# wo and w1 in long rows, and a quarter of one wo block moved into mid-run, in a decode kernel of attention and a Mish MLP

## The chip, the cores and the metric

One core of a Trainium2 chip runs the kernel. The metric is the device time of one execution in microseconds. A core has a matrix engine (TensorE, PE in the profile, with its weight loads as PEld), a vector engine (VectorE, DVE), a scalar engine (ScalarE, ACT), GpSimd (POOL) and SyncE (SP), which here issues nearly all transfers. Sixteen DMA engines carry the data from HBM into SBUF, whose 128 partitions the engines read; results of matmuls land in PSUM.

## The reference, cut to what matters

One token for each of 8 sequences (B = 8) passes a layer norm, and then two branches side by side: grouped-query attention over a cache (32 query heads, 8 key/value heads, 8192 positions, head size 128), and a dense layer of 1792 with Mish and a dense layer back. Everything is float32.

```python
xn = _layernorm(x, axis=-1)                       # x: 8 x 1 x 512
q = (xn @ wq).reshape(B, Sq, 32, 128)             # wq: 512 x 4096
scores = q . k_cache * 128 ** -0.5                # k_cache, v_cache: 8 x 8 x 8192 x 128
o = softmax(scores) . v_cache
A = o.reshape(B, Sq, 4096) @ wo                   # wo: 4096 x 512
h = xn @ w1 + b1                                  # w1: 512 x 1792
M = (h * tanh(softplus(h))) @ w2                  # w2: 1792 x 512
return x + A + M
```

## The kernel before

The work is cut into 32 units. Unit j is one batch row b = j % 8 with one pair m = j // 8 of key/value heads (NP = 4 pairs). A unit has 8.39 MB of keys and as many of values, and each of these is one transfer of 128 rows of 64 KiB (`load_unit`). The query projection of a pair, `project`, needs a quarter of wq, which `load_q` brings into the 16 KiB tile `ws`; it is loaded at b = 4 of the pair before and used at b = 5.

One large tile `kv` holds everything else. Values lie in its first 64 KiB of each partition (V_AT). Keys of even and odd units lie in two 64 KiB places that overlap by half (K_AT), so that the keys of unit j + 1 may be issued when one half of the scores of unit j has been computed. w1, the input x and the scratch of the Mish part share the first key place (W1_AT). K0, the first unit's keys, is loaded to the place of the values, so V0 must wait for the scores of unit 0, and K2 must wait for the Mish scratch to be free.

The program is written in the order in which each engine runs it (a manual schedule): every engine takes its instructions in program order and waits on semaphores where it needs another's result. At the start come the constants, the layer norm on 8 partitions (lines 169 to 183), eight small transposes of the normalised x into PSUM tile `M` (lines 184 to 189: four with stride 4 for the projection, `xn4`; four of 128 neighbouring columns for w1, `xnT`), their copies out, four matmuls that spread x for the residual (line 193), then the projection of pair 0, `spread` and the key weights of unit 0.

The loop over units then does, for unit j: the scores (line 279) in two halves with the next keys' transfer issued between them; the softmax (`softmax`); the values of unit j - 1 (`values`, line 341) on the probabilities that were turned in the iteration before; the transfer of V_j, which overwrites V_(j-1) and so follows `values(j - 1)`; the key weights of unit j + 1; for j = 0 `mish`; for some j `load_q` and `project`; `turn`, which permutes the exponentials with matmuls and lets DVE transpose and reduce them into `pt8` (lines 318 to 329); and `merge(j - 1)`, which scales the output of unit j - 1 and puts it into `oT` (lines 358 and 359). SP's issues are in the same order: K_(j+1), V_j, wq if it is due. A matmul in float32 appears as two matmul entries and two weight-load entries in the profile. Matmuls whose results go to the four quarters of PSUM's partitions, as most here do, run four at a time.

`mish` adds b1 and multiplies x by w1 (line 370: 4 blocks of 128 input rows times 4 groups of 448 columns), applies Mish with 14 vector operations in a chain, and leaves the turned result in `aT` (line 404).

After the loop SP issues wo as four transfers of 2 MiB (one for each pair, lines 477 to 480: 128 partitions times four rows of 4 KiB) and w2 as four (line 486). PE computes the values of the last unit, then `outputs(m, ...)` for three pairs (line 413: 8 matmuls for each pair, straight from `oT`), `merge` of the last unit and the outputs of the fourth pair. ACT copies the sum out of PSUM, four matmuls fold it (line 497), `down` adds the product with w2 (line 425), DVE adds x, and one transfer writes the result.

Of the kernel before, what the change touches and what calls it, by code (L numbers as in the profile page):

```python
# [13 lines left out]
P = 128  # L14
# [35 lines left out]

W2R = 7
# [7 lines left out]
PLACES = 2 * ROW + ROW // 2  # L59

# [5 lines left out]
def kernel(  # L66
# [39 lines left out]
    xnT = const.tile([P, CC, B], F32, name="xnT")  # L106
    qr = const.tile([P, DI, H2 * B], F32, name="qr")
    xres = const.tile([P, P], F32, name="xres")
    oT = const.tile([P, NP, H2, B], F32, name="oT")
# [20 lines left out]
    low = kv[:B, W1_AT : W1_AT + 3 * D]  # L130
    x_sb, xc, sq = (low[:, i * D : (i + 1) * D] for i in range(3))
# [5 lines left out]
    w1_t = kv[:, W1_AT : W1_AT + 7168].rearrange("p (j f) -> p j f", j=2 * CC)  # L137
# [5 lines left out]
    nc.gpsimd.memset(pt8, 0.0)  # L143
    for t in (H, O, M):
        nc.vector.memset(t, 0.0)
# [7 lines left out]
    nc.vector.reduce_sum(bsel, ident.rearrange("p (g q) -> p q g", g=G), axis=AX.X)  # L153
    nc.vector.reduce_sum(hsel, ident.rearrange("p (c h) -> p h c", h=H2), axis=AX.X)
# [29 lines left out]
    for c in range(CC):  # L184
        nc.tensor.transpose(M[:, c * B : (c + 1) * B], xc[:, c::CC], ident[:B, :B])
    for c in range(CC):
        nc.tensor.transpose(
            M[:, 32 + c * B : 32 + (c + 1) * B], xc[:, c * P : (c + 1) * P], ident[:B, :B]
        )
    nc.vector.tensor_copy(xn4.rearrange("p c b -> p (c b)"), M[:, 0:32])  # L190
    nc.vector.tensor_copy(xnT.rearrange("p c b -> p (c b)"), M[:, 32:64])
# [21 lines left out]
    def project():  # L213

        w = ws.rearrange("p (c f) -> p c f", c=CC)
        for d in range(2):
# [8 lines left out]
            qp = work.tile([P, 512], F32, name="e")  # L225
# [63 lines left out]
    def softmax(j):  # L289
# [18 lines left out]
        e = E[j] = work.tile([P, 512], F32, name="e")  # L308
# [47 lines left out]
    def merge(j, os):  # L356
        m, b = divmod(j, B)
        nc.tensor.matmul(M[:, 168 : 168 + H2], os, hsel, start=True, stop=True)  # L358
        nc.vector.tensor_mul(oT[:, m, :, b], M[:, 168 : 168 + H2], RT.pop(j))


    def mish(w1_t, b1_sb, flat):
# [5 lines left out]
        for c in range(CC):  # L368
            for g in range(G):
                nc.tensor.matmul(  # L370
                    hp[Q * g : Q * g + B, :],
                    xnT[:, c, :],
                    w1_t[:, c * 2 + g // 2, g % 2 * FG : (g % 2 + 1) * FG],
                    start=False,
                    stop=(c == CC - 1),
# [31 lines left out]
    A = X[:, 0]  # L407

    def outputs(m, t):
        w = t.rearrange("p (u f) -> p u f", u=4)  # L410
        for d in range(2):
            for h in range(REP):
                nc.tensor.matmul(
                    A[Q * h : Q * h + B, :],
                    oT[:, m, d * REP + h, :],
                    w[:, d * 2 + h // 2, h % 2 * D : (h % 2 + 1) * D],
                    start=(m == 0 and d == 0),
                    stop=(m == NP - 1 and d == 1),
                )

    def down(lo, hi, w):
        for j in range(2 * lo, 2 * hi):
            for g in range(G):
                at = (j - 2 * lo) * D + g * P
                nc.tensor.matmul(
                    H[Q * g : Q * g + B, :P],
# [7 lines left out]
    nc.sync.dma_start(w1_t, w1.rearrange("j p f -> p j f"))  # L434
# [6 lines left out]
    for j in range(UNITS):  # L441
# [20 lines left out]
        if j == 0:  # L462
            mish(w1_t, b1_sb, kv[:, W1_AT : W1_AT + 6 * FG])
        if more and b == LOAD_Q:
            load_q(j // B + 1)
        if more and b == MAKE_Q:
            qT = project()
        turn(j, lsel)
        if j > 0:
            merge(j - 1, os)  # L470
        if more and b == SPREAD_Q - 1:
            selections()


    w_o = [kv[:, 4096 * m : 4096 * (m + 1)] for m in range(NP)]
    for m in range(NP):
        nc.sync.dma_start(
            w_o[m].rearrange("p (u f) -> p u f", u=4),
            wo[4 * m : 4 * (m + 1)].rearrange("u p f -> p u f"),
        )  # L480
    w2_rows = w2.rearrange("j p f -> (j p) f").rearrange("(q i) f -> q (i f)", i=W2R)
    w2_t = []
    parts = ((0, 2), (2, 4), (4, 6), (6, 7))
    for lo, hi in parts:
        t = kv[:, W2_AT + lo * BW : W2_AT + hi * BW]
        nc.sync.dma_start(t, w2_rows[:, lo * BW : hi * BW])  # L486
# [60 lines left out]
```

## Time and profile before

| | |
|---|---|
| median of 3 runs (lowest to highest) | 1312.56 us (1312.44 to 1312.78) |
| the profiled execution, its own time | 1312.45 us |
| its span, first to last instruction | 1310.7 us |
| busy: PE / DVE / ACT | 989.0 us (75%) / 515.1 us (39%) / 40.2 us (3%) |
| read from HBM | 561.01 MB, 428 GB/s over the span |
| mean granted clock of TensorE | 0.879 of full speed |

In the rows of the profile an instruction is named by its engine, the line of the program, the operation and `out<-in` with the tiles' names; then come partitions x elements and a count. In a timeline the first number is the start in us from the span's start, the second the duration, and in brackets stands how long the engine was idle before and what ended that. In the windows a row has a stretch of time, its length, the busy time (and number) of PE, PEld, DVE, ACT and POOL, the granted TensorE clock, the mean busy share of the 16 DMA engines, and GB/s. A share over 1 in a short window comes from packets that are counted where they begin. SPq stands for SP's queue of DMA issues.

### The profile page before, as it was taken

Reading aid. Unit: us, or ns where it says so; the run is one execution under the profiler, and the core shown is the slowest. Engines: PE = TensorE matmul, PEld = TensorE weight load, DVE = VectorE, ACT = ScalarE, POOL = GpSimd, SP = SyncE. Lnnn points to the kernel's source line nnn. Section 1 sums busy time; section 2 is a strip of 40 time slices with the busy share of each in tenths; the row PEclk is TensorE's granted clock in tenths of the full one; section 3 lists DMA queues with packets and bytes.
Section 4 is the critical chain, followed back from the end, with each engine's and each line's share of the span. In section 5 each row is a group of like instructions: output and inputs, shape, how many; then the busy total and the mean of one; then the engine's idle time right before and its main releaser. Section 6 shows DMA issues by size and latency. Waiting matters only on the chain.

```text
span 1310.7 us, 11149 instructions
## 1 busy us (share of the span) xinstructions
PE 989.0 (75%) x5040; PEld 340.5 (26%) x5040; DVE 515.1 (39%) x728; ACT 40.2 (3%) x88; POOL 2.2 (0%) x9
## 2 busy tenths in 40 slices
PE   5978867768877668777878777687686678677676
PEld 3222222222322222232322222232232222222222
DVE  3364334432444442335243344414444433344421
ACT  1000000000000000000000000000000000000000
POOL 0000000000000000000000000000000000000000
PEclk9988888898888888877888888888898898888898
DMA  9999999999999999999999999999999999999997
GB/s 393 451 422 439 427 436 430 432 439 429 441 429 433 431 437 425 447 415 447 423 439 433 427 441 423 443 425 439 429 435 431 435 431 437 432 435 421 441 414 322
DMA packets 13735, 561.79 MB, mean 429 GB/s; under 512 B 1260, under 2 KB 1392, under 8 KB 4600
## 3 DMA queue, kind: packets, MB, share of 16 engines
q1 hardware_dynamic: 13664, 561.06, 99.3%
q8 instruction: 39, 0.64, 0.2%
q10 hardware_dynamic: 24, 0.02, 0.0%
q14 instruction: 8, 0.07, 0.0%
HBM read 561.01 MB, written 0.07 MB: 428 GB/s over the span
## 4 chain that ended last, share of the span: by engine, by line
DMA 72%; PE 23%; DVE 2%; SPq 2%; issue 0%; ACT 0%; DVEq 0%
DMA kv<-in_v 71%; PE o L341 20%; SPq L486 1%; DMA kv<-in_w 1%; PE s L279 1%; DVE pt L329 1%; PE x L244 1%; PE h L370 0%; PE m L229 0%; PE h L218 0%; DVE kv L392 0%; DVE tr L323 0%; DVE wk L262 0%; DVE nm L291 0%; ACT L177 0%
## 5 line engine op out<-in xcount | busy, mean ns | idle before, releaser
L279 PE MATMUL s<-kv,wk 128*64 128x512 f32 x2048 | 504.4, 655 | 174.6 <-DMA kv<-in_kT 171.9
L341 PE MATMUL o<-kv,pt 128*32 128x512 f32 x2048 | 268.6, 684 | 54.9 <-DMA kv<-in_v 45.3
L279 PEld LDWEIGHTS s<-kv,wk 128*64 128x64 f32 x2048 | 155.6, 151 | 498.0 <-issue 320.6
L329 DVE TENSOR_REDUCE pt<-tr 64x512 f32<-64x2048 f32 x64 | 241.3, 3771 | 1.6
L291 DVE TENSOR_REDUCE nm<-s 128x1 f32<-128x512 f32 x32 | 22.1, 691 | 366.7 <-PE s L279 366.7
L318 PE MATMUL x<-e,perm 128*128 128x512 f32 x256 | 128.4, 648 | 2.0 <-ACT qr L251 2.0
L341 PEld LDWEIGHTS o<-kv,pt 128*32 128x32 f32 x2048 | 69.9, 123 | 227.1 <-issue 169.6
L349 DVE TENSOR_SCALAR os<-o,isel 128x128 f32<-128x128 f32 x32 | 11.2, 351 | 274.8 <-PE o L341 274.8
L323 DVE STREAM_TRANSPOSE tr<-x 128x512 f32<-128x512 f32 x128 | 78.7, 673 | 0.0
L262 DVE TENSOR_TENSOR wk<-qr,mask 128x512 f32<-128x512 f32 x64 | 63.0, 1026 | 19.7 <-ACT qr L251 19.7
L318 PEld LDWEIGHTS x<-e,perm 128*128 128x128 f32 x256 | 50.0, 206 | 76.2 <-issue 73.7
L310 ACT ACTIVATE e<-s,nmx 128x512 f32<-128x512 f32 x32 | 22.0, 687 | 1095.7 <-DVE nmx L307 1095.7
L351 DVE SCALAR_TENSOR_TENSOR os<-o,isel,os 128x128 f32<-128x128 f32 x96 | 33.7, 351 | 3.4
L292 PE MATMUL m<-ident,nm 128*1 128x128 f32 x32 | 8.7, 273 | 29.8 <-DVE nm L291 29.8
L303 PE MATMUL m<-ident,nx 1*128 1x1 f32 x32 | 7.0, 219 | 24.1 <-DVE nx L299 24.1
L244 PE MATMUL x<-qT,tr 128*128 128x64 f32 x128 | 19.3, 315 | 3.0 <-ACT qr L251 2.7
L321 DVE RECIPROCAL rt<-m 128x8 f32<-128x8 f32 x32 | 6.6, 207 | 36.1 <-PE m L319 36.1
L244 PEld LDWEIGHTS x<-qT,tr 128*128 128x128 f32 x128 | 18.1, 226 | 6.2 <-ACT qr L251 3.3
L358 PE MATMUL m<-hsel,os 128*128 128x8 f32 x64 | 12.4, 266 | 9.3 <-DVE rt L321 9.3
L312 DVE TENSOR_SCALAR lsel<-rsel,l 128x8 f32<-128x8 f32 x32 | 7.4, 231 | 30.1 <-ACT e L310 30.1
L292 PEld LDWEIGHTS m<-ident,nm 128*1 128x1 f32 x32 | 2.5, 79 | 58.0 <-DVE nm L291 58.0
L319 PEld LDWEIGHTS m<-lsel,ones 128*128 128x128 f32 x64 | 12.2, 190 | 15.4 <-issue 15.1
(88 smaller groups left out, 163.9 us busy)
## 6 DMA issues: line engine op xcount, KB each, us to landing
ws<-in_wq SPq DMA_DIRECT2D x4, 2048.0 KB, 34.3
kv<-in_wo SPq DMA_DIRECT2D x4, 2048.0 KB, 24.3
kv<-in_w SPq DMA_DIRECT2D x1, 3584.0 KB, 26.4
kv<-in_w SPq DMA_DIRECT2D x3, 1024.0 KB, 19.3
kv<-in_kT SPq DMA_DIRECT2D x32, 29.9
kv<-in_v SPq DMA_DIRECT2D x32, 30.2
kv<-in_w SPq DMA_DIRECT2D x1, 512.0 KB, 19.5
out<-os SPq DMA_DIRECT2D x1, 64.0 KB, 1.6
```

The source lines that it names most:

```text
L244: nc.tensor.matmul(X[:, half, k * 64 : (k + 1) * 64], wide[:, half * 8 + k], qT, start=True, stop=True,)
L262: nc.vector.tensor_mul(w[:, :, d], q[:, :, d].to_broadcast([P, DI, NH * G, REP]), mask[:, d * NH * G : (d + 1) * NH * G] .rearrange("p (o ...
L279: nc.tensor.matmul(S[64 * c : 64 * (c + 1), :], w[:, i].rearrange("p d k h -> p (d k h)"), kk[:, i, c, :], start=(part == 0 and n == 0), s ...
L291: nc.vector.tensor_reduce(nm, S, axis=AX.X, op=ALU.max, negate=True)
L310: nc.scalar.activation(e, S, AF.Exp, bias=nmx, accum_out=l)
L318: nc.tensor.matmul(X[:, g], perm[:, g], e, start=True, stop=True)
L323: nc.vector.transpose(tr.rearrange("p (l t) c -> p t l c", t=TL)[:, tl], X.rearrange("p g (t q l) -> p t l g q", t=TL, q=PP)[:, tl],)
L329: nc.vector.tensor_reduce(pt8[half, :, :, d * REP : (d + 1) * REP].rearrange("p c y h -> p y c h"), tr[half].rearrange("p y (g c h) -> p y ...
L341: nc.tensor.matmul(O[Q * q : Q * (q + 1), :], pt8[:, c, TL * l : TL * (l + 1), :].rearrange("p t h -> p (t h)"), vt[:, 512 * n : 512 * (n ...
L351: nc.vector.scalar_tensor_tensor(os, O[:, DH * i : DH * (i + 1)], isel[:, i : i + 1], os, op0=ALU.mult, op1=ALU.add)
L358: nc.tensor.matmul(M[:, 168 : 168 + H2], os, hsel, start=True, stop=True)
L486: nc.sync.dma_start(t, w2_rows[:, lo * BW : hi * BW])
```

## The change

wo: the four transfers now read the same 2 MiB blocks as one run of memory, so that each partition gets one row of 16 KiB. A partition then holds four neighbouring rows of a block instead of row p of each of four, and the attention output must lie on the partitions in the same order: the new `turn_o(m)` does that for a pair with 16 matmuls by slices of the identity and one copy, `oT` into `oX`. For the first pair the row has 12 KiB only. The missing quarter (512 KiB) comes into `ws` by twelve transfers in mid-run (`load_few`): eight of three rows of 16 KiB at j = 22 to 25, to partitions p, p + 4 and p + 8 with p = 0 to 3 and 32 to 35, and four of two rows at j = 28 and 29, to partitions 0 to 7. Their matmuls are `few(0)` at the end of iteration 27 and `few(1)` after the last values; `turn_few` lays out their side of the product once, after unit 7. All of these add into PSUM tile `H`, which takes the place of `X` as accumulator of the outputs; the product with w2 goes to `O` in place of `H`.

w1: each partition reads one run of 28 KiB, eight rows of 896. The input must match: x is copied on 8 partitions into a new order (`xe`), turned by eight transposes and masked into two halves (`x8`), and `mish` has 32 matmuls for w1 where it had 16.

w2 comes in five parts (three of 8 KiB a partition, two of 2 KiB) in place of four. The work tile "e" has one buffer in place of two, and `project` comes after `turn` and `merge` in its iteration.

```diff
+W1R = 8
+FEW1 = [(32 * h + t, 3, 12 * h + t, 22 + (4 * h + t) // 2) for h in range(2) for t in range(4)]
+FEW2 = [(t, 2, 24 + t, 28 + t // 2) for t in range(4)]
+EARLY = 27
...
+    xe = kv[:B, W1_AT + 3 * D : W1_AT + 3 * D + W1R * P].rearrange("b (i s) -> b i s", i=W1R)
...
     for c in range(CC):
         nc.tensor.transpose(M[:, c * B : (c + 1) * B], xc[:, c::CC], ident[:B, :B])
+    nc.vector.tensor_copy(xn4.rearrange("p c b -> p (c b)"), M[:, 0:32])
     for c in range(CC):
-        nc.tensor.transpose(
-            M[:, 32 + c * B : 32 + (c + 1) * B], xc[:, c * P : (c + 1) * P], ident[:B, :B]
-        )
-    nc.vector.tensor_copy(xn4.rearrange("p c b -> p (c b)"), M[:, 0:32])
-    nc.vector.tensor_copy(xnT.rearrange("p c b -> p (c b)"), M[:, 32:64])
+        nc.vector.tensor_copy(
+            xe.rearrange("b i (c h q) -> b c i h q", c=CC, h=2)[:, c],
+            xc[:, c * P : (c + 1) * P]
+            .rearrange("b (o q i) -> b i o q", o=1, i=W1R)
+            .to_broadcast([B, W1R, 2, P // CC // 2]),
+        )
+    for i in range(W1R):
+        nc.tensor.transpose(M[:, 32 + i * B : 32 + (i + 1) * B], xe[:, i], ident[:B, :B])
+    for h in range(2):
+        nc.vector.tensor_scalar(
+            x8[:, :, h],
+            M[:, 32 : 32 + W1R * B].rearrange("p (i b) -> p i b", i=W1R),
+            hmask[:, h : h + 1],
+            None,
+            op0=ALU.mult,
+        )
...
-        nc.vector.tensor_mul(oT[:, m, :, b], M[:, 168 : 168 + H2], RT.pop(j))
+        nc.vector.tensor_mul(oT[:, :, b], M[:, 168 : 168 + H2], RT.pop(j))
+        if b == B - 1:
+            turn_o(m)
+        if j == B - 1:
+            turn_few()
+
+    def turn_o(m):
+        for i in range(CC):
+            for u in range(CC):
+                nc.tensor.matmul(
+                    M[Q * u : Q * (u + 1), 256 + 2 * B * i : 256 + 2 * B * (i + 1)],
+                    ident[:, i::CC],
+                    oT[:, 2 * u : 2 * u + 2].rearrange("p h b -> p (h b)"),
+                    start=True,
+                    stop=True,
+                )
+        nc.vector.tensor_copy(
+            oX[:, m].rearrange("p i h b -> p (i h b)"), M[:, 256 : 256 + 2 * CC * B]
+        )
...
-        for c in range(CC):
+        for i in range(W1R):
             for g in range(G):
                 nc.tensor.matmul(
                     hp[Q * g : Q * g + B, :],
-                    xnT[:, c, :],
-                    w1_t[:, c * 2 + g // 2, g % 2 * FG : (g % 2 + 1) * FG],
+                    x8[:, i, g // 2],
+                    w1_t[:, i, g % 2 * FG : (g % 2 + 1) * FG],
...
+    def load_few(p, n, q):
+        rows = wo[:4].rearrange("u p f -> (u p f)").rearrange("(u q i f) -> q u i f", u=4, i=4, f=BW)
+        nc.sync.dma_start(
+            ws[p : p + 4 * n - 3 : 4].rearrange("p (u f) -> p u f", u=4),
+            rows[q : q + 4 * n - 3 : 4, :, 3],
+        )
+
+    def turn_few():
+        o = oT.rearrange("p h b -> p (h b)")
+        n = H2 * B
+        for k, (p, m, lo) in enumerate(((0, 12, 0), (32, 12, 12), (0, 8, 24))):
+            part = k // 2
+            nc.tensor.matmul(
+                M[p : p + m, 384 + n * part : 384 + n * (part + 1)],
+                ident[:, 4 * lo + 3 : 4 * (lo + m) : 4],
+                o,
+                start=True,
+                stop=True,
+            )
+            nc.vector.tensor_copy(
+                oF[p : p + m, part].rearrange("p u h b -> p (u h b)"),
+                M[p : p + m, 384 + n * part : 384 + n * (part + 1)],
+            )
+
+    def few(part):
+        rows = (44, 8)[part]
+        for n in range(2 * CC):
+            nc.tensor.matmul(
+                H[Q * (n % G) : Q * (n % G) + B, :],
+                oF[:rows, part, n // 2, n % 2],
+                ws[:rows, n * D : (n + 1) * D],
+                start=(part == 0 and n < G),
+                stop=False,
+            )
...
-    nc.sync.dma_start(w1_t, w1.rearrange("j p f -> p j f"))
+    nc.sync.dma_start(w1_t, w1.rearrange("j p f -> (j p f)").rearrange("(p i f) -> p i f", p=P, i=W1R))
...
+        for p, n, q, at in FEW1 + FEW2:
+            if j == at:
+                load_few(p, n, q)
         if more and b == LOAD_Q:
             load_q(j // B + 1)
-        if more and b == MAKE_Q:
-            qT = project()
         turn(j, lsel)
         if j > 0:
             merge(j - 1, os)
+        if more and b == MAKE_Q:
+            qT = project()
         if more and b == SPREAD_Q - 1:
             selections()
+        if j == EARLY:
+            few(0)
...
-        nc.sync.dma_start(
-            w_o[m].rearrange("p (u f) -> p u f", u=4),
-            wo[4 * m : 4 * (m + 1)].rearrange("u p f -> p u f"),
-        )
+        rows = wo[4 * m : 4 * (m + 1)].rearrange("u p f -> (u p f)")
+        rows = rows.rearrange("(p f) -> p f", p=P)
+        n = 3 * BW if m == 0 else 4 * BW
+        nc.sync.dma_start(w_o[m][:, :n], rows[:, :n])
...
-    parts = ((0, 2), (2, 4), (4, 6), (6, 7))
+    parts = ((0, 4), (4, 8), (8, 12), (12, 13), (13, 14))
...
     os = values(UNITS - 1, v_t.pop(UNITS - 1))
+    few(1)
     for m in range(NP - 1):
         outputs(m, w_o[m])
     merge(UNITS - 1, os)
     outputs(NP - 1, w_o[NP - 1])
```

60 lines of the change are left out of this document (33 added, 27 removed).

## The prediction

> **What bounds the kernel now.** I read the page first, then the DMA share and rate by windows.
>
> ```profile
> span 1310.7 us, 11149 instructions
> ...
> q8 instruction: 39, 0.64, 0.2%
> ...
> DMA 72%; PE 23%; DVE 2%; SPq 2%; issue 0%; ACT 0%; DVEq 0%
> ...
> kv<-in_v SPq DMA_DIRECT2D x32, 30.2
> ```
>
> The chain that ended last is 72% DMA. Its 20% on L341 is a bookkeeping effect: while a unit's values run, the next keys are already moving. The windows decide (share of 16 engines, then GB/s):
>
> ```profile
> 200.00:400.00 200.00, 158.30 (x786) 54.82 (x781) 78.60 (x107) 6.23 (x14) 0.00 (x0) 0.86 1.00 433
> 29.00:35.00 6.00, 3.68 (x10) 1.21 (x12) 1.94 (x2) 0.29 (x1) 0.00 (x0) 1.00 1.03 412
> 1284.00:1296.00 12.00, 12.00 (x104) 2.88 (x96) 1.40 (x4) 0.00 (x0) 0.00 (x0) 0.89 1.03 412
> 1300.00:1301.00 1.00, 0.63 (x8) 0.00 (x0) 0.00 (x0) 0.26 (x1) 0.00 (x0) 1.00 0.58 242
> 1305.00:1306.00 1.00, 0.00 (x0) 0.00 (x0) 0.00 (x0) 0.00 (x0) 0.00 (x0) 1.00 0.34 139
> ```
>
> In mid-run all 16 engines are full at 433 GB/s (27.1 each). The stages with short rows are full too, but carry 412: w1 (29 to 35 us) and wo (1284 to 1296). In the last stretch only 0.58 of the engines work, so nine of the 16 end later than the other seven, by most of the time between 1299 and 1306: about 7 us. The 39 instruction packets of 16 KB are the only unequal load the page shows; 7 us against 39/9 of them is 1.6 us of lag for each. That cause is inferred. So the end is set by the late engines' bytes, and by any moment at which their queue is empty.
>
> **The change, part by part.** The times below are those of the profiled execution: 1312.45 us, 0.11 below the median of the three runs shown (1312.56), with 1.75 us outside its span.
>
> **Rows and the moved quarter: -2.1 us of transfers at the end, -0.4 at the start.** wo is 8.39 MB: at 412 GB/s 20.4 us. Afterwards 7.86 MB remain there; in 12 and 16 KiB rows at 433 that is 18.2 us (-2.2; if longer rows brought nothing, 7.86/412 is 19.1, -1.3). w1's 3.67 MB go from 8.9 to 8.5 us. w2's last 4 KiB part becomes two of 2 KiB: 0.1 us more at worst, since its four parts become five.
>
> **The few rows.** 512 KB go in twelve transfers. If each row has its own engine, two engines take twelve rows of 16 KiB (192 KB) and one takes eight. At 25.8 GB/s (412/16) 192 KB is 7.6 us. That is free as long as those engines are among the early seven with their 7 us; the excess of 0.6 us, less what the idle time below evens out, is taken as +0.5 (0 to 0.8). Their issues cost SP twelve times 0.33 us, in its idle time.
>
> **Start of the run: layer norm to w1.** Read the PE rows, and the DVE rows next to them:
>
> ```profile
> 9.96 0.57 PE L187 MATMUL m<-ident,kv 8*128 8x8 f32 x4
> 10.91 0.61 PE L193 MATMUL m<-kv,ident 8*8 8x128 f32 x8 [0.38 <-DVE xnT L191]
> ```
>
> ```profile
> 8.87 0.47 DVE L183 TENSOR_SCALAR kv<-kv,st 8x512 f32<-8x512 f32 x1
> 10.57 0.19 DVE L190 COPY xn<-m 128x32 f32<-128x32 f32 x1 [1.23 <-PE m L187]
> ```
>
> L193 waits for DVE's last read of M, and the projection is queued behind it. New in that path are four copies of 8x256 (between 0.19 and 0.47 each; near 0.3 as half of L183's elements, 1.2 in all), eight transposes in place of four, now after the copies and not beside them (0.11 to 0.14 each, 1.0), and two masked copies of 128x64 (0.2 each) where one copy stood. L190 itself comes after four transposes, not eight (-0.5). Sum about +2.0 us (1.3 to 3.0) for projection, spread and scores(0).
>
> **mish.** Sixteen more matmuls, 32 more entries:
>
> ```profile
> 51.10 4.79 PE L370 MATMUL h<-kv,xnT 128*8 128x448 f32 x32
> ...
> 79.93 9.62 PE L341 MATMUL o<-kv,pt 128*32 128x512 f32 x64
> ```
>
> ```profile
> 51.00:54.00 3.00, 2.90 (x16) 0.59 (x20) 0.50 0.81 350
> 54.00:55.90 1.90, 1.89 (x20) 0.36 (x12) 0.90 1.28 552
> ```
>
> The first 16 entries ran at a granted clock of 0.50 (0.18 us each), the rest at 0.90 (0.095). The new ones come last, so 32 x 0.095 = 3.0 us; at the low clock throughout 5.8. The bounds of the whole delay are thus 4.3 and 8.8, and I take 2.0 + 3.0 = 5.0.
>
> **Who waits for that.** K2 overwrites mish's scratch, and V1 overwrites V0:
>
> ```profile
> 67.46 0.22 DVE L404 COPY aT<-kv 128x112 f32<-128x112 f32 x1
> ```
>
> ```profile
> 67.75 0.33 SPq L123 DMA_DIRECT2D kv<-in_kT  x1
> 89.61 0.33 SPq L123 DMA_DIRECT2D kv<-in_v  x1
> ```
>
> K2 is issued when L404 ends. In DVE's order turn(0) and the maximum of unit 1 come next; values(0) needs both (L341, 79.93 to 89.55, 12.3 us after L404's end), and V1 is issued behind it. The 5 us therefore reach both: K2 at 72.8, V1 at 94.6. When is the queue empty? Ahead of V1 stand wq 2.10, K0 8.39, w1 3.67, K1, V0 and K2 with 8.39 each: 39.3 MB, 90.8 us at 433, from about 2.3 on: 93.1, and up to 1 us more with the slow stages; I take 94. What an issue into a nearly empty queue costs shows late in the run, at its first row:
>
> ```profile
> 1171.70 0.33 SPq L123 DMA_DIRECT2D kv<-in_kT  x1
> 1189.92 0.33 SPq L123 DMA_DIRECT2D kv<-in_v  x1
> 1209.83 0.33 SPq L123 DMA_DIRECT2D kv<-in_kT  x1
> ```
>
> ```profile
> 1172.50:1173.00 0.50, 0.50 (x6) 0.14 (x2) 0.00 (x0) 0.00 (x0) 0.00 (x0) 1.00 0.00 0
> 1173.00:1173.50 0.50, 0.50 (x4) 0.14 (x2) 0.00 (x0) 0.00 (x0) 0.00 (x0) 1.00 2.13 786
> ```
>
> No packet begins before 1173.0: 1.3 to 1.8 us after the issue; with 1.7, V1's begin at 96.3. So the engines stand still for 2.3 us once, and w1's 0.4 us is lost in it. K2's own gap (72.8 + 1.7 against about 74) lies inside that. By then only about three of the 39 fetches have come, so most engines that are late at the end have no lag yet that could hide it: **+2.3 us** (1.6 to 6.1). The Trainium skill (DMA: Bandwidth & Descriptors, Latency and other measured facts) gives 0.6 us to the first byte of a transfer issued from SP; by it V1 would begin at 95.2 and the sum be 1.1 us lower, 1312.4. The row above speaks against it.
>
> **turn_o, few(0), project in mid-run.** turn_o waits on PE for L359, ahead of the next scores:
>
> ```profile
> 1239.49 15.29 PE L279 MATMUL s<-kv,wk 128*64 128x512 f32 x64 [7.85 <-DMA kv<-in_kT]
> ...
> 1241.19 0.17 DVE L359 TENSOR_TENSOR oT<-m,rt 128x8 f32<-128x8 f32 x1
> ```
>
> Scores at j = 9, 17 and 25 start 1.7 us later plus turn_o's own 1.1 (at j = 9 also turn_few's three rounds of matmul and copy, about 1.7). Late engines do not feel it: the next K issue has the V transfer queued ahead of it. few(0)'s 1.7 us lie in PE's 7.85 us of idle time. project after turn and merge keeps its place ahead of the next scores. The one buffer for e is free by then: L318 has read it. All 0; without the queued V it would be 2.8 us three times.
>
> **The tail on PE.** Here a second path comes up:
>
> ```profile
> 1290.97 5.32 PE L413 MATMUL x<-kv,oT 128*8 128x512 f32 x48
> 1296.22 0.39 PE L358 MATMUL m<-hsel,os 128*128 128x8 f32 x2
> 1298.73 1.90 PE L413 MATMUL x<-kv,oT 128*8 128x512 f32 x16 [2.12 <-DMA kv<-in_wo]
> 1301.38 0.41 PE L497 MATMUL h<-e,bsel 128*8 128x128 f32 x8 [0.74 <-ACT e L495]
> 1301.60 1.06 PE L425 MATMUL h<-kv,aT 128*8 128x128 f32 x32
> ...
> 1307.28 0.62 PE L425 MATMUL h<-kv,aT 128*8 128x128 f32 x16 [0.17 <-DMA kv<-in_w]
> ```
>
> Now PE waits for the last wo (2.12 us) and for w2. Afterwards few(1) adds eight matmuls (16 entries at 5.32/48, 1.7 us) and outputs(0) saves two, which gains nothing as they stand half-filled in their groups of four. merge(31) moves to 1297.9, oT to 1298.5; turn_o(3)'s 32 entries take about 1.1 (as L425's, with narrower moving data but wider weights; 0.5 to 4), its copy with both waits 0.4, outputs(3) 1.9: 1301.9 against 1300.6. To the first L425 another 0.97 as now: 1302.9. The 112 entries, no longer interrupted, are 3.2 us: **1306.1, against 1307.9 now: -1.8.** The transfers would allow 1307.28 - 2.1 + 0.4 = 1305.6, so PE sets the end and 0.5 us of the transfer gain is lost.
>
> **Sum:** 2.3 - 1.8 + 0.5 = +1.0, and 1312.45 + 1.0 = 1313.45: **1313.4 us**, no change that can be told (a measurement of this kernel tells some 0.2%, 2.6 us).
>
> **Rivals.**
> A, *the start hides*: if copies and transposes overlap more than I grant, or V1's queue lasts, the idle time is under 0.5 us. For it: 94 is known to 1 us. Against: from L370 to V1's issue every step waits for the one before. Then -0.4 - 1.8 gives 1310.2, and 1309.4 if turn_o is nearly free and the transfers end the run.
> B, *SP stands at the second few transfer* (the other side): the rows of a pair interleave in the same 12 partitions of ws. If the second waits for the first to land, SP holds K behind it until about 30 us after V's issue (median landing 30.2), where K now goes out at 20 (1189.92 to 1209.83). It decides from 28.5 on (30.2 - 1.7): then all engines idle some 2.5 us in four of the six steps, once the three engines' lead is used up: 1323. Against it: the rows share no byte.
> C, *no lead on those engines*: were they among the late nine, 7.6 us come on top and the 0.5 falls away: 1320.5. The trace does not number engines, so nothing here excludes it. The Trainium skill (DMA: Bandwidth & Descriptors, Why a DMA increments its semaphore by 16 and not by 1) says a transfer of three rows runs on the three lowest-numbered engines only; no run here shows that yet.
> D, *mish stays at the low clock*: +2.8, 1316.2.
>
> **How the numbers follow.** Chances: forecast 0.45, A 0.25, B 0.12, C 0.08, D 0.10. The forecast's own range is 1311 to 1315. The whole range, 1309.3 to 1317, takes in A and D and leaves out B and C. Faster by over 0.2% (under 1309.9): most of A's lower half and a little of the forecast, 0.19. Slower (over 1315.2): B, C, D and 0.03 of the forecast, 0.33. Within: 0.48.
>
> **What would show it.** Right: V1's issue near 94.6 with a window of low DMA share just before 96; L370 near 7.8 us; L425 without DMA waits; the share in the last 7 us near 0.7 or more. Wrong: V1 issued before 92 (A), K issues 30 us behind V at j = 22 to 29 (B), a last stretch of three engines alone (C), L370 over 9.5 us (D).

## The result, and the profile after

| | before | after |
|---|---|---|
| median of the runs (lowest to highest) | 1312.51 us (1312.36 to 1313.33, 12 runs) | 1315.62 us (1314.06 to 1318.60, 12 runs) |
| ratio to before, 95% interval | | 1.0025 (1.0018 to 1.0033) |
| the profiled execution | 1312.45 us | 1314.06 us |
| its span | 1310.7 us | 1312.2 us |
| highest less lowest | 0.97 us | 4.54 us |

The change costs 3.1 us. The forecast was 1313.4 us (range 1309.3 to 1317.0). The profiled execution is the fastest of the twelve, so it shows less than the usual loss. What a single profile can't show at all is the last row: the changed kernel varies almost five times as much.

From the page of the changed kernel come the span, the chain and two groups of instructions (count, busy us, mean ns, then the idle time just before them and what ended it). The helpers' lines have moved: L224 was L193, L310 was L279, L372 was L341, L420 was L370, L498 was L413, L510 was L425.

```profile
span 1312.2 us, 11581 instructions
...
DMA 54%; PE 35%; DVE 9%; issue 1%; ACT 1%; ACTq 0%; DVEq 0%
...
L260 PE MATMUL m<-bsel,e 128*128 128x8 f32 x64 | 14.9, 362 | 30.4 <-DVE oT L390 26.7
...
L400 PE MATMUL m<-oT,ident 128*32 128x16 f32 x128 | 2.7, 220 | 29.6 <-DVE oT L390 29.6
```

The chain was 72% DMA and is 54%. The two groups are new waits: the projection stands 26.7 us in all, and turn_o 29.6 us, behind L390, the product that `merge` leaves to DVE. The timelines of PE around two of them, from the changed kernel first and then from the one before, show what that does:

```profile
255.28 1.84 PE L260 MATMUL m<-bsel,e 128*128 128x8 f32 x8 [8.90 <-DVE oT L390]
...
261.51 1.12 PE L310 MATMUL s<-kv,wk 128*64 128x512 f32 x2
...
377.56 0.68 PE L400 MATMUL m<-oT,ident 128*32 128x16 f32 x32 [9.78 <-DVE oT L390]
...
380.39 4.54 PE L310 MATMUL s<-kv,wk 128*64 128x512 f32 x10
```

```profile
255.96 2.83 PE L279 MATMUL s<-kv,wk 128*64 128x512 f32 x6 [3.98 <-DMA kv<-in_kT]
...
373.61 2.83 PE L279 MATMUL s<-kv,wk 128*64 128x512 f32 x6 [6.14 <-DMA kv<-in_kT]
```

Before, the scores of these units waited for their keys. Now the keys lie there and the scores start 5.6 us later (261.51) and 6.8 us later (380.39), because PE stands behind DVE's transposes and reductions. DVE's own rows for the second place say why it takes so long:

```profile
367.26 2.46 DVE L354 STREAM_TRANSPOSE tr<-x 128x512 f32<-128x512 f32 x4
369.75 7.55 DVE L360 TENSOR_REDUCE pt<-tr 64x512 f32<-64x2048 f32 x2
377.34 0.17 DVE L390 TENSOR_TENSOR oT<-m,rt 128x8 f32<-128x8 f32 x1
```

L390 is a product of 0.17 us that stands in DVE's order behind 10 us of `turn`. SP issues the next keys in the middle of the scores. SP's own rows, changed kernel and then before, are V5 and K7, then V8 and K10:

```profile
241.03 0.33 SPq L135 DMA_DIRECT2D kv<-in_v  x1
270.96 0.33 SPq L135 DMA_DIRECT2D kv<-in_kT  x1
...
363.42 0.33 SPq L135 DMA_DIRECT2D kv<-in_v  x1
390.13 0.33 SPq L135 DMA_DIRECT2D kv<-in_kT  x1
```

```profile
240.54 0.33 SPq L123 DMA_DIRECT2D kv<-in_v  x1
264.67 0.33 SPq L123 DMA_DIRECT2D kv<-in_kT  x1
...
363.09 0.33 SPq L123 DMA_DIRECT2D kv<-in_v  x1
383.22 0.33 SPq L123 DMA_DIRECT2D kv<-in_kT  x1
```

Both keys are issued more than 6 us later. Whether anything is lost by that is seen in the windows (the last two columns are the share of the 16 DMA engines and GB/s). First the changed kernel, then before:

```profile
94.00:96.00 2.00, 2.00 (x6) 0.95 (x5) 2.00 (x3) 0.00 (x0) 0.00 (x0) 1.00 0.59 229
392.00:394.00 2.00, 2.00 (x12) 0.70 (x10) 0.00 (x0) 0.00 (x0) 0.00 (x0) 1.00 0.40 164
1300.00:1301.00 1.00, 1.00 (x12) 0.19 (x4) 0.00 (x0) 0.00 (x0) 0.00 (x0) 1.00 1.03 426
```

```profile
94.00:96.00 2.00, 0.00 (x0) 0.00 (x0) 1.97 (x5) 0.00 (x0) 0.00 (x0) 0.83 0.83 360
392.00:394.00 2.00, 1.11 (x9) 0.38 (x12) 0.39 (x2) 0.78 (x2) 0.00 (x0) 0.57 0.83 360
```

At the start (94 to 96) and around K10's late issue (392 to 394) the share is lower than before. In windows of 2 us a packet counts where it begins, so neither 0.40 nor the 0.83 of before tells how many engines stood idle. The traces also give the begin and the duration of every packet, and where fewer than sixteen are in flight, an engine stands still. Counted so, as a mean of the sixteen engines, 0.3 us are lost between 93 and 95 us and 0.7 us between 389 and 393. From 40 to 1230 us it is 1.7 us in all, against 0.2 in the kernel before. The third row is the other side of it: between 1300 and 1301 the share is 1.03, where it was 0.58. The seven engines that used to finish 7 us early don't finish as early any more. Part of that lead was spent by standing still.

Then the tail on PE, in the changed kernel, with the one row of before from which it is counted:

```profile
1261.73 8.77 PE L372 MATMUL o<-kv,pt 128*32 128x512 f32 x64 [1.65 <-DMA kv<-in_v]
1284.51 9.89 PE L372 MATMUL o<-kv,pt 128*32 128x512 f32 x64 [9.57 <-DVE pt L360]
...
1305.97 3.24 PE L510 MATMUL o<-kv,aT 128*8 128x128 f32 x112
```

```profile
1258.84 8.77 PE L341 MATMUL o<-kv,pt 128*32 128x512 f32 x64 [2.03 <-DMA kv<-in_v]
```

values(30) is the last place where PE waits for V. From there to the last matmul it is 1309.21 - 1261.73 = 47.5 us, against 1307.90 - 1258.84 = 49.1 before. The tail became 1.6 us shorter, and L510 runs without a wait, as forecast. V30 came 2.9 us later.

### The profile page after: what moved, and what is told of

The parts are those of the page before. It is cut to its first block, busy times and chain, and to the rows that moved or that the text cites. A ratio compares the mean times of both kernels' runs of the same rounds, so it can differ in the third digit from the quotient of the medians.

```text
span 1312.2 us, 11581 instructions
## 1 busy us (share of the span) xinstructions
PE 996.2 (76%) x5238; PEld 346.8 (26%) x5238; DVE 518.5 (40%) x741; ACT 40.2 (3%) x88; POOL 2.3 (0%) x10
## 4 chain that ended last, share of the span: by engine, by line
DMA 54%; PE 35%; DVE 9%; issue 1%; ACT 1%; ACTq 0%; DVEq 0%
DMA kv<-in_v 54%; PE o L372 20%; PE s L310 9%; DVE pt L360 5%; PE x L349 2%; DVE tr L354 1%; PE m L260 1%; PE h L249 1%; PE x L275 1%; PE h L498 1%; PE h L420 0%; DVE nm L322 0%; PE o L510 0%; ACT e L257 0%; DVE kv L442 0%
## 5 line engine op out<-in xcount | busy, mean ns | idle before, releaser
L310 PE MATMUL s<-kv,wk 128*64 128x512 f32 x2048 | 506.9, 658 | 126.5 <-DMA kv<-in_kT 123.9
L372 PE MATMUL o<-kv,pt 128*32 128x512 f32 x2048 | 262.3, 671 | 44.2 <-DMA kv<-in_v 34.7
L310 PEld LDWEIGHTS s<-kv,wk 128*64 128x64 f32 x2048 | 156.4, 152 | 452.1 <-issue 322.5
L349 PE MATMUL x<-e,perm 128*128 128x512 f32 x256 | 124.8, 632 | 2.0 <-ACT qr L282 2.0
L372 PEld LDWEIGHTS o<-kv,pt 128*32 128x32 f32 x2048 | 68.9, 121 | 210.9 <-issue 164.4
L341 ACT ACTIVATE e<-s,nmx 128x512 f32<-128x512 f32 x32 | 22.0, 687 | 1055.7 <-DVE nmx L338 1055.7
L260 PE MATMUL m<-bsel,e 128*128 128x8 f32 x64 | 14.9, 362 | 30.4 <-DVE oT L390 26.7
L260 PEld LDWEIGHTS m<-bsel,e 128*128 128x128 f32 x64 | 14.2, 327 | 42.0 <-issue 29.4
L334 PE MATMUL m<-ident,nx 1*128 1x1 f32 x32 | 7.0, 219 | 24.1 <-DVE nx L330 24.1
L400 PE MATMUL m<-oT,ident 128*32 128x16 f32 x128 | 2.7, 220 | 29.6 <-DVE oT L390 29.6
## 6 DMA issues: line engine op xcount, KB each, us to landing
kv<-in_wo SPq DMA_DIRECT2D x3, 2048.0 KB, 24.1
```

What stands on the lines that cost most here:

```text
L260: nc.tensor.matmul(M[:, at : at + B], qp[:, h * DH : (h + 1) * DH], bsel[:, :B], start=True, stop=True,)
L310: nc.tensor.matmul(S[64 * c : 64 * (c + 1), :], w[:, i].rearrange("p d k h -> p (d k h)"), kk[:, i, c, :], start=(part == 0 and n == 0), s ...
L341: nc.scalar.activation(e, S, AF.Exp, bias=nmx, accum_out=l)
L349: nc.tensor.matmul(X[:, g], perm[:, g], e, start=True, stop=True)
L372: nc.tensor.matmul(O[Q * q : Q * (q + 1), :], pt8[:, c, TL * l : TL * (l + 1), :].rearrange("p t h -> p (t h)"), vt[:, 512 * n : 512 * (n ...
```

## The experiments

Three causes stood against each other for the late V30 and for the spread. S: only the start, where mish holds V1's issue back. M: the order in mid-run. F: the few rows, which land on engines that are late. All runs below were timed beside the kernel before (medians 1312.49 to 1312.54 us).

**The changed kernel again.**

> The changed kernel once more, unchanged, for a second profile and its spread. In its first profile the last packet of V30 (issued at 1230.57) released values(30) at 1261.73, against 1258.84 in the kernel before, and from there to the last matmul it took 47.5 us (49.1 before). Theory M (the keys are issued late in mid-run): the late issues at j = 5, 8, 13, 16, 21 and 24, 24 to 30 us behind V, come again in the same places, since they follow from the order of the program; V30 again releases values(30) 1 to 4 us later than before. Theory S (only the start is late, 2.3 us, as I had forecast): V1 is issued near 93 and nothing is lost after it. Both: 1314 to 1318 us, and values(30) moves with the total while the 47.5 us stay within 0.3.

Measured: 1316.78 us (1313.94 to 1317.86), 1.0028 (1.0016 to 1.0040). values(30), and the share in two late windows:

```profile
1264.58 1.90 PE L372 MATMUL o<-kv,pt 128*32 128x512 f32 x12 [1.77 <-DMA kv<-in_v]
```

```profile
392.00:394.00 2.00, 2.00 (x12) 0.70 (x10) 0.00 (x0) 0.00 (x0) 0.00 (x0) 1.00 0.25 98
...
1308.00:1309.00 1.00, 0.52 (x20) 0.52 (x24) 0.00 (x0) 0.42 (x1) 0.00 (x0) 1.00 0.12 49
```

V30 is 5.7 us late this time, beyond the 1 to 4 us expected, and the gap at K10 is in the same place and deeper (1.4 us by the packets in flight, where it was 0.7). At the very end the share is 0.12. Two of 16 engines are 0.125, and the trace has two packets in flight there: two engines are still working when the other fourteen have finished. S falls: V1 was issued 0.6 us earlier than in the first profile (92.2 against 92.8), and V30 came 2.9 us later.

**Without the few rows.** All of wo comes at the end.

```diff
-        for p, n, q, at in FEW1 + FEW2:
-            if j == at:
-                load_few(p, n, q)
...
-        if j == EARLY:
-            few(0)
...
-    few(1)
...
-        n = 3 * BW if m == 0 else 4 * BW
+        n = 4 * BW
```

> The few rows are taken out whole: no transfers to ws in mid-run, no few(0), few(1), turn_few; wo comes as four transfers of 16 KiB rows at the end. Theory F (the two engines that carry the last few rows are themselves the late ones by V30, so that their 4 x 16 KB of j = 28 and 29, 2.4 us, arrive late one for one): values(30) starts 1.5 to 2.4 us earlier than in the changed kernel, near 1259.5, and the total is 1311 to 1312.3 us (few(1)'s 1.9 us go from the tail, 1.2 us of wo come back into its transfers). Theory M: the lateness of V30 stays at 1 to 3 us, as the order of mid-run is unchanged; the total falls only by the tail, 1312.5 to 1315. The forecast's step (excess of 0.5 us): V30 0.5 earlier.

Measured: 1313.62 us (1311.82 to 1314.75), 1.0007 (0.9997 to 1.0016): 2.0 us less than the changed kernel's 1315.62, and 3.2 less than its six executions just above. The total lies in the range of theory M, not in that of F. Its one profile can't decide the place, because there the start went badly (mish took 7.53 us, V1 went out at 95.0) and values(30) still began at 1261.60.

**Mid-run order as it was, and then both edits.**

```diff
-            qp = work.tile([P, 512], F32, name="e", bufs=1)
+            qp = tr.rearrange("p y c -> p (y c)")[:, :512]
...
-        if b == B - 1:
-            turn_o(m)
-        if j == B - 1:
-            turn_few()
+        if j == UNITS - 1:
+            turn_o(m)
...
+        if j > B and b == 1:
+            turn_o(j // B - 1)
+            if j == B + 1:
+                turn_few()
         for p, n, q, at in FEW1 + FEW2:
...
+        if more and b == MAKE_Q:
+            qT = project()
         turn(j, lsel)
         if j > 0:
             merge(j - 1, os)
-        if more and b == MAKE_Q:
-            qT = project()
```

In these two kernels the first projection writes over the selection matrices as well, so that q is not the reference's; instructions, sizes and order are those shown.

> The changed kernel with the mid-run order put right: project before turn, as in the kernel before (its copy of H goes to the idle tr), and turn_o(0..2) and turn_few one unit later, behind values, when oT has long been written. Few rows, start and tail stay. Theory M (project and turn_o stand behind DVE's turn, 9 us six times, the keys are issued 3 to 7 us late and the early engines run dry): the key issues return to 24 to 27 us behind V at j = 5, 13, 21 and to about 20 at j = 8, 16, 24; no DMA share under 0.7 over 2 us near 392; the early engines keep their lead, so the few rows fit into it; values(30) at 1259 to 1259.5; total 1311.0 to 1312.0 us with a spread under 1.5 us. Theory F alone: V30 still 2 us or more late and 1313.5 to 1315. Theory S: no change, 1314 to 1318.

Measured: 1314.17 us (1310.88 to 1315.91), 1.0006 (0.9997 to 1.0016). The keys were on time (24.1 us behind V at j = 5, 19.9 at j = 8), but the spread stayed at 5.0 us and the median fell only 1.4. The expected 1311 to 1312 came in single runs alone, and the median lies where theory F alone had put it: a second cause was left.

> Both edits: no few rows, project before turn, turn_o one unit later. Left of the change are the long rows of wo and w1, the start, mish and the tail's turn_o(3). Theory M or F: values(30) at 1259.0 to 1259.5 (0.4 us for the start), from there a tail without few(1); the transfers end it: wo's and w2's 12.06 MB... 1.3 to 2 us shorter than before, total 1310.7 to 1311.8 us. Theory S: values(30) still 2 to 3 us late, 1312.5 to 1313.5.

Measured: 1313.81 us (1312.14 to 1316.10), 1.0010 (1.0001 to 1.0019). Not 1310.7 to 1311.8, and values(30) began at 1262.47. The profile shows the second cause. PE's row for mish, then windows over it and at V1's issue (95.89):

```profile
54.02 9.03 PE L418 MATMUL h<-kv,x 128*8 128x448 f32 x64
```

```profile
54.00:58.50 4.50, 4.50 (x32) 0.94 (x32) 1.86 (x2) 0.00 (x0) 0.00 (x0) 0.50 1.08 466
...
94.00:96.00 2.00, 2.00 (x21) 0.54 (x14) 0.10 (x1) 0.00 (x0) 0.00 (x0) 1.00 0.08 33
```

Half of mish ran at a granted clock of 0.50, and it took 9.03 us where the changed kernel's first profile has 6.20. V1 was issued 3 us later than there, and for 2 us nearly all engines stood still (0.08).

**The start alone put back, and with it the rest.**

```diff
-    x8 = const.tile([P, W1R, 2, B], F32, name="x8")
+    xnT = const.tile([P, CC, B], F32, name="xnT")
...
-        for i in range(W1R):
+        for c in range(CC):
...
-                    x8[:, i, g // 2],
-                    w1_t[:, i, g % 2 * FG : (g % 2 + 1) * FG],
+                    xnT[:, c, :],
+                    w1_t[:, c * 2 + g // 2, g % 2 * FG : (g % 2 + 1) * FG],
```

> The changed kernel with only the start put back: w1 in 8 transfers' worth of 3.5 KB rows as before, xnT and 32 matmuls of mish in place of xe, x8 and 64. Theory P (mish has twice the matmuls and runs 6.2 to 9.0 us by the clock it is granted, so V1 is issued between 92.2 and 95.9, from within to 3 us beyond the end of its queue; the spread of the times comes from there): V1 issued near 89.6, no idle DMA before 120 us, the spread falls from 4.5 us to under 2; the mid-run losses stay, 1312.3 to 1314 us. Rival Q (the spread comes from where the late key issues and the instruction fetches fall in mid-run): spread still 4 us or more, median 1314 to 1315.5.

Measured: 1314.49 us (1313.78 to 1316.43), 1.0015 (1.0006 to 1.0024). V1 at 89.3, as in the kernel before (89.6), and 1.1 us gained; the spread fell to 2.65 us, between what P and Q expected, and the median lies in the range of Q. V30 was still late, and the two engines were there again:

```profile
1264.28 1.92 PE L355 MATMUL o<-kv,pt 128*32 128x512 f32 x16 [1.53 <-DMA kv<-in_v]
```

```profile
1308.00:1309.00 1.00, 0.02 (x3) 0.00 (x0) 0.00 (x0) 0.00 (x0) 0.00 (x0) 1.00 0.10 43
```

The next kernel adds the mid-run order; only the first projection still uses e:

```diff
+            if first:
+                qp = work.tile([P, 512], F32, name="e", bufs=1)
+            else:
+                qp = tr.rearrange("p y c -> p (y c)")[:, :512]
```

> The start put back, project before turn again (its copy of H in tr, except the first one), turn_o(0..2) and turn_few one unit later; few rows, long rows of wo and the tail stay. Theory P with M: V1 issued near 89.6, key issues as in the kernel before, the early engines keep their lead and the few rows fit into it; values(30) at 1258.5 to 1259.5, from there 47.5 us; total 1310.3 to 1311.5 us, spread under 1.5 us, faster than both kernels. Rival Q: 1312 to 1314 with a spread of 4 us.

Measured: **1311.17 us** (1310.75 to 1311.47), 0.9989 (0.9980 to 0.9998), and a spread of 0.7 us. values(30):

```profile
1259.38 2.67 PE L358 MATMUL o<-kv,pt 128*32 128x512 f32 x9 [0.48 <-DMA kv<-in_v]
```

V30 comes 0.5 us later than in the kernel before.

> As the run before it, and without the few rows (wo whole at the end in 16 KiB rows). Left of the change: the rows of wo, oX and the tail. If the few rows cost nothing once the early engines have their lead, this one is slower or equal by what its transfers carry more at the end (0.5 MB, 1.2 us): 1311.0 to 1312.0 us, with waits of the last matmuls on DMA. If the few rows still land late (theory F), it is faster than the run before it by 0.5 to 2 us.

Measured: 1311.64 us (1311.45 to 1312.11), 0.9993 (0.9984 to 1.0002): 0.5 us slower. With the keys on time the few rows are a gain.

**The kernel before with the new start alone** (the diff of the start, the other way round). A first version without the room described below needed 10.16 KB of work tiles in each partition, where 9.81 KB were left, so there is no time for it.

> The kernel before with only the new start: w1 in one 28 KiB row for each partition, xe, x8, 64 matmuls of mish (to make room, e has one buffer and project's later copies of H go to tr, which cost nothing measurable in the run that beat both kernels). Theory P (mish's clock decides how far V1's issue lies behind the end of its queue): mish 6.2 to 9 us, V1 issued 92 to 96, the DMA idle 0.2 to 3 us in all between 40 and 120 us; median 1313 to 1315 us, spread 3 to 5 us, where the kernel before has 1. Rival Q (the spread comes from late keys and fetches in mid-run): within 0.5 us of the kernel before, spread about 1 us.

Measured: 1313.88 us (1312.55 to 1316.63), 1.0013 (1.0004 to 1.0021), spread 4.1 us. In its profile, again, half of mish at 0.50 (L391 is mish) and DMA that stands still before V1, which was issued at 95.60:

```profile
53.60 9.12 PE L391 MATMUL h<-kv,x 128*8 128x448 f32 x64
```

```profile
53.60:58.10 4.50, 4.50 (x32) 0.96 (x32) 2.08 (x3) 1.13 (x3) 0.00 (x0) 0.50 1.08 466
...
94.00:96.00 2.00, 2.00 (x18) 0.55 (x10) 0.35 (x2) 0.00 (x0) 0.00 (x0) 1.00 0.03 8
```

V1 is not the only late issue here. K2 waits for the end of mish too, and the engines stand still longer before K2 (1.4 us between 74 and 77, by the packets in flight) than before V1 (0.9 us):

```profile
74.58 0.33 SPq L125 DMA_DIRECT2D kv<-in_kT  x1
```

```profile
74.00:75.50 1.50, 1.50 (x10) 0.47 (x8) 1.47 (x5) 0.00 (x0) 0.00 (x0) 1.00 0.00 0
75.50:76.00 0.50, 0.50 (x6) 0.21 (x4) 0.50 (x2) 0.00 (x0) 0.00 (x0) 1.00 4.72 1573
```

**The two halves of mid-run, and the few rows under late keys.** All three have the old start. The first has project early and turn_o in merge, the second turn_o late and project behind merge, the third the order of the change and no few rows.

> Old start, project before turn again; turn_o and turn_few stay in merge, few rows stay. It splits the 3.3 us between 1314.5 (old start alone) and 1311.2 (old start and both orders). If turn_o with turn_few behind DVE's turn at j = 8, 16, 24 is most of it (the one stretch of 40 us with 0.7 us of mean idle was at 360 to 400, j = 8): 1313.3 to 1314.5 us. If project at j = 5, 13, 21 is most of it: 1311.2 to 1312.3.

> Old start, turn_o(0..2) and turn_few one unit later; project stays behind turn and merge, few rows stay. The other half of the same split: if turn_o is most of it, 1311.2 to 1312.4 us; if project is, 1313.3 to 1314.5. The two halves need not add up, because an engine that has idled once has less lead to lose.

> Old start, mid-run order as in the change, without the few rows. Theory F with M (idle time in mid-run takes the lead of the engines that carry the few rows, and these then land last: in the run with the old start V30's last two engines came 3.3 us behind the next one): without them V30 lands 2 to 3 us earlier, values(30) at 1261 to 1262, total 1312 to 1313 us against 1314.5. If the few rows are innocent and the idle time alone delays V30: values(30) stays near 1264 and the total is 1314 to 1315.5 us. With the keys on time, the few rows were worth 0.5 us.

Measured: 1312.80 us (1311.62 to 1314.25), 1.0003 (0.9994 to 1.0011); 1314.46 us (1312.78 to 1316.82), 1.0015 (1.0006 to 1.0024); and 1311.55 us (1311.39 to 1313.54), 0.9995 (0.9986 to 1.0004). The project's three late places alone cost as much (3.3 us over 1311.17) as all six; the three of turn_o alone cost 1.6. My bet on turn_o was the wrong one. The third run came out lower than either theory had it (1312 to 1313 or 1314 to 1315.5). In the second run, values(30) and the end, and in the third, values(30):

```profile
1264.71 1.85 PE L355 MATMUL o<-kv,pt 128*32 128x512 f32 x12 [1.75 <-DMA kv<-in_v]
```

```profile
1308.00:1309.00 1.00, 0.36 (x16) 0.36 (x20) 0.00 (x0) 0.58 (x1) 0.00 (x0) 1.00 0.11 45
```

```profile
1258.78 2.90 PE L355 MATMUL o<-kv,pt 128*32 128x512 f32 x16 [1.85 <-DMA kv<-in_v]
```

Without the few rows V30 is on time, late keys or not. So neither the late keys nor the few rows are at fault by themselves. With the old start, four medians say it:

| us | with few rows | without |
|---|---|---|
| keys on time | 1311.17 | 1311.64 |
| keys late | 1314.49 | 1311.55 |

What the late keys take away can be counted by the packets in flight, again as a mean of the sixteen engines. Mid-run is 110 to 1230 us here; the last column compares each profile's values(30) with 1258.84. Each row of the experiments is one execution, and those with 5.4, 5.9 and 3.2 are the slowest or next to slowest of their eleven:

| us | idle, 40 to 110 | idle in mid-run | values(30) later by |
|---|---|---|---|
| the kernel before | 0.0 | 0.2 | |
| the change, two profiles | 0.4 and 0.1 | 1.3 and 2.0 | 2.9 and 5.7 |
| old start, keys on time, few rows | 0.0 | 0.2 | 0.5 |
| old start, only turn_o's keys late, few rows | 0.0 | 1.1 | 2.0 |
| old start, all six keys late, few rows | 0.0 | 1.3 | 5.4 |
| old start, only the project's keys late, few rows | 0.0 | 1.5 | 5.9 |
| old start, all six keys late, no few rows | 0.0 | 0.9 | -0.1 |
| kernel before with the new start | 2.3 | 0.2 | 3.2 |

Engines stand still in mid-run only where keys are late, and each time around the issue of a late key, at one to three of the places in each profile. A rough estimate of the size: seven early engines that bear 0.9, 1.1 and 1.3 us alone (1.1, 1.3 and 1.5 less the 0.2 of the kernel before) lose 16/7 of that each, 2.1 to 3.0 us of their 7. The few rows' 7.6 us would then overrun the lead by 2.7 to 3.6 us. V30 came 2.0 to 5.9 us late: the order of size is right, and the rest of it is not accounted for.

**few(1) in PE's gap**, in the fastest of these kernels.

```diff
+    few(1)
     os = values(UNITS - 1, v_t.pop(UNITS - 1))
-    few(1)
```

> The run that beat both kernels (old start, project early, turn_o late, few rows) with few(1) moved ahead of values(31), into the 9.58 us in which PE waits there for DVE's last reduction. If PE alone sets the end, its 1.9 us go whole: 1309.3 us. In that run's profile the transfers' share falls to 0.32 between 1304 and 1305 and to 0.02 after 1305, so w2 lands near 1305.1; behind that the last 16 or 48 of down's entries (0.6 to 1.7 us) must still run, and the last matmul, now at 1306.35, can end no earlier than about 1305.7 to 1306.0. By that the gain is 0.3 to 0.7 us: 1310.4 to 1310.9, with L494 waiting for the transfer of w2 again.

Measured: **1310.76 us** (1310.54 to 1310.89), 0.9986 (0.9977 to 0.9995), another 0.4 us:

```profile
1272.43 1.90 PE L470 MATMUL h<-ws,oF 8*8 8x512 f32 x16
1282.07 9.60 PE L358 MATMUL o<-kv,pt 128*32 128x512 f32 x64 [7.75 <-DVE pt L346]
...
1304.39 1.69 PE L494 MATMUL o<-kv,aT 128*8 128x128 f32 x48 [1.13 <-DMA kv<-in_w]
```

few(1) now lies in the wait for DVE, and the last matmuls wait for w2 again: the transfers are the bound once more. This version is 1.7 us faster than the kernel before and 4.9 us faster than the change.

## Why the forecast came out as it did, step by step

Taken apart by medians with the old start as the hinge: 1312.51 to 1311.17 is -1.3 for the long rows of wo, the few rows and the tail; 1311.17 to 1314.49 is +3.3 for the order in mid-run; 1314.49 to 1315.62 is +1.1 for the start. The sum is +3.1; the forecast had -1.3 (-1.8 + 0.5), 0 and +2.3. The six further executions of the changed kernel have 1316.78, and over all eighteen its median is 1316.4. The start's share is therefore known only as 1.1 to 1.9.

- **Rows, 412 to 433 GB/s: half of it came.** The changed kernel moves wo at 425 GB/s in the window where the kernel before has 412:

```profile
1284.00:1296.00 12.00, 11.49 (x80) 2.67 (x80) 2.04 (x6) 0.00 (x0) 0.00 (x0) 0.74 1.01 425
```

By that the remaining 7.86 MB take 18.5 us and not 18.2. PE sets the end of the changed kernel, so nothing of its total hangs on this.

- **The tail, -1.8, and the few rows, +0.5: right**, where their conditions held. With the keys on time V30 is 0.5 us late (1259.38 against 1258.84) and the total 1.3 us lower. PE sets the end, as forecast; the 0.5 us less that the transfers would allow are what the last run collected (0.4).
- **"turn_o, few(0), project in mid-run: All 0": this step failed.** Two things were wrong in it. "project after turn and merge keeps its place ahead of the next scores" is true on PE's list and passes over DVE's: behind merge, the projection's writes to M wait for L390's read of M, and L390 stands behind 10 us of turn. For turn_o at j = 8 I had 1.7 + 1.1 + 1.7 = 4.5 us of delay for the scores, where they start 6.8 us later. I had taken the 1.7 from unit 31. At unit 8 of the kernel before the keys were there at 373.61, 3.4 us ahead of its L359:

```profile
377.02 0.17 DVE L359 TENSOR_TENSOR oT<-m,rt 128x8 f32<-128x8 f32 x1
```

The second error is the one that cost time. "Late engines do not feel it" agrees with the run without few rows (old start, V30 at 1258.78). But the early engines do feel it, and the step for the few rows had just lent out their lead. I asked of each edit whether it has cover, and gave both the same cover: 7 us of lead. Late keys spend it in idle time; then the few rows, up to 7.6 us of work on few engines, come on top of engines that are less early, and V30 waits for the last two.
- **The start, +2.3: mechanism right, but its size is no single number, and one term was misread.** The forecast took 1.7 us from an issue to its first packet, from a window at 1172.5 in which no packet begins. But the sixteen engines were busy there with packets of 2.4 us that had begun earlier. Where they did stand still, the first packets began 0.95 to 0.97 us after the issue (K2 at 74.58 and V1 at 95.60 in the kernel before with the new start, K2 at 74.91 and V1 at 95.89 in the run with both edits), and the other engines' within about 2 us. So 1.0 us is the better term for the first engine, and the 0.6 us that the forecast set aside on the strength of that row is nearer than 1.7. V1's issue was put at 94.6; the profiles have 92.8, 92.2, 95.0, 93.0, 95.9 and 95.6. The four matmuls ahead of the projection came 2.5 us later (13.40 against 10.91; forecast 2.0), and mish's 64 entries took 6.20 us when the clock stayed at 1.00 and 9.03 or 9.12 when about half of them had 0.50 (forecast 7.8). V1 stands at the edge of its queue and K2 close to it, so the first costs little (0.1 to 0.4 us of idle engines between 40 and 110 us) and the second 2.3 to 2.6. By medians the new start costs 1.1 to 1.9 us on top of the late keys, 1.4 in the kernel before, and 3.0 (1314.17 against 1311.17) where all else is on time. That these differ would follow if idle time in different places is partly the same time lost, as engines that have waited once have less to lose later; this is argued and not measured.
- **The rivals.** A (the start hides) did not come. B (SP stands at the second few transfer) did not come: in the changed kernel V28, a pair of few transfers in 1.36 us, and the keys 20 us behind V:

```profile
1151.89 0.33 SPq L135 DMA_DIRECT2D kv<-in_v  x1
1152.27 1.36 SPq L460 DMA_DIRECT2D ws<-in_wo  x2
1171.97 0.33 SPq L135 DMA_DIRECT2D kv<-in_kT  x1
```

- C (no lead on those engines) came by a way I had not listed: the lead was there and was spent. It showed as two engines at the end, not three: the last transfers are those of two rows, four of them. The Trainium skill (DMA: Bandwidth & Descriptors, Why a DMA increments its semaphore by 16 and not by 1) has a transfer run on as many engines as its rows divide into, up to 16, and on the lowest-numbered of the sixteen; the share of 0.10 to 0.12, two engines of 16, agrees in number, and no row here shows which they are. D (mish at the low clock) came in part, in some executions: 9.03 and 9.12 us, short of the 9.5 set as its sign, because the low clock ended within mish. It is most of the spread where the keys are on time: with the order put right, 0.7 us with the old start and 5.0 with the new one. Late keys with few rows bring a spread of their own, 2.6 to 4.0 us with the old start. There the engines stand still at other late keys from profile to profile; what picks the place was not traced.

So it was luck that the time came out inside the whole range. It lies outside the forecast's own 1311 to 1315, among the outcomes called slower (over 1315.2, chance 0.33), and the whole range covers it only because it takes in D, which is not what made most of the loss. Two errors partly cancel: the mid-run step was put at 0 and cost 3.3, and the start was put at 2.3 and cost 1.1 to 1.9. By the median shown first the forecast was 2.2 us low; with the start at its measured +1.1 it would have been 3.4 low.

## What to carry to other kernels

Slack that several edits lean on is one budget: when a transfer is hidden by an engine's lead and another edit lets that engine run dry, add them up before calling either free, and test them together. Before an instruction is moved behind another on its engine, look at what the other one waits for on every engine's list; here a product of 0.17 us held PE for 9 us or more because DVE had 10 us queued in front of it. A work item whose granted clock varies belongs where there is slack for its slow case, and a spread of 4 us in place of 1 is a sign that it stands at an edge.

## What the runs showed of the hardware

The clock under mish was not a property of the kernel. In the six profiles of kernels with the new start, the same 64 entries ran at 1.00 throughout in three (6.20 us each) and partly at 0.50 in the others (7.53, 9.03 and 9.12 us), though PE had just finished 15 to 17 us of scores and had paused for only 0.80 and 0.76 us. The rows are those of the runs without the few rows (7.53 us) and with both edits (9.03 us):

```profile
53.00:56.30 3.30, 3.30 (x24) 0.59 (x20) 1.37 (x3) 1.88 (x3) 0.00 (x0) 0.50 0.74 318
```

```profile
54.02:59.70 5.68, 5.68 (x36) 1.22 (x36) 1.84 (x2) 0.00 (x0) 0.00 (x0) 0.50 0.99 427
59.80:63.00 3.20, 3.20 (x37) 0.72 (x29) 0.00 (x0) 0.00 (x0) 0.00 (x0) 1.00 1.05 451
```

The clock's own entries in the traces show what differs. In each of the 14 traces all changes of the clock lie whole multiples of 3.41 us apart, from the first to the last. So the clock changes only at the edges of windows of that length. The low clock around mish lasts one window in the first of these profiles (52.97 to 56.38) and two in the second (52.94 to 59.77). The two pauses before mish add up to 1.55 us in every profile, with the old start too. In the eight profiles where both fell into one window, the next window ran at 0.50; in the six where an edge parted them, with at most 1.29 us in one window, it ran at 1.00. What differs from run to run is thus where the edges fall. This is a pattern at one place of 14 profiles; no run moved the pauses to test it, and why the low clock then lasts one window or two stays open. The Trainium skill (TensorE: Matmul & The Clock Gate, What's actually happening) describes a window of activity of some 3.4 us that runs free of the kernel, after which the clock is halved or restored; the traces agree with the window's length and with the variation from run to run. The Trainium skill names an idle window there as the condition for half speed, while here a window with 1.55 us of pauses, less than half of it, was enough.
